# Top-k attention with a squared-ReLU MLP on one core: the first pair's loads and transposes, the timing of the weight loads, and identity products on TensorE

## The chip, the cores and the metric

One core of one Trainium2 chip runs the whole program. The metric is the device time of one execution in microseconds (us); the kernel before took 872.97 us, the median of three runs (872.86 to 874.77). The profile comes from one further execution of 870.8 us, whose traced span is 869.0 us. The engines are called as the profile calls them: PE (TensorE; PEld is its weight load), DVE (VectorE), ACT (ScalarE), POOL (GpSimd) and SP (SyncE, which here only issues DMAs).

## The reference

```python
# q, k, v: (8, 8, 576, 64) float32
scores = q @ k.transpose / sqrt(64)
kth = the 32nd largest score of each row
attn = softmax of the scores >= kth, the others left out
x = (attn @ v), heads side by side: (4608, 512)
h = x @ w_in            # (512, 2048)
out = relu(h)**2 @ w_out    # (2048, 512) -> (4608, 512) float32
```

## The kernel before, in words

**Tiles.** Two heads make a *pair*; there are 8 batches of 4 pairs. A pair's q and k (576 rows each) are loaded as 128-row blocks with the two heads side by side (tiles rq and rk; four whole blocks and a rest of 64 rows, three DMAs each). PE transposes them (ten transposes, L447), and ACT copies the result from PSUM into one tile qk (L511 to L514). A *group* is 128 queries of both heads of a pair (or 64 rests of two pairs); there are 144 groups. For each group:

- PE makes the scores (eight matmuls, L444) in a three-bank PSUM buffer of which there is one, ps_s.
- ACT copies them to SBUF (tile s, L555), DVE takes pairwise maxima (three operations, L611 and L621, called the *pair operations* here), partly reading ps_s; PE's next scores wait for the second of them. One quarter of the maxima lies for a moment in another single PSUM buffer, ps_q, which ACT empties (L619).
- POOL makes the matching minima by integer additions and subtractions (L606).
- DVE finds the 32nd largest by rounds of eight maxima and replacements (L638, L642, last L645, which writes kth).
- ACT makes a steep ReLU mask w (L653), PE transposes the scores and adds the mask (nine transposes and nine matmuls, called *flips* here), ACT takes the exponential p (L687), PE multiplies with v (tile vb, which POOL casts from rv at L515), ACT, DVE and POOL divide by the sum, and PE transposes the result into xt. The ninth block of the flips lies in ps_q too.

When all heads of 128 or 256 tokens are there, the MLP of this chunk is run: win matmuls, ReLU on ACT (L768), square on POOL, ACT or, for the last chunk, DVE (L779), wo matmuls, and an output DMA of 256 KB (L810).

**Weights.** w_in and w_out come as 16 float32 loads of 512 KB on SP's queue (L891) into two staging buffers, and are cast to bf16 by ACT or POOL (L894). All 16 may start from 6 us of the plan on (WN); how far apart they then come is set by their due times and the two buffers.

**Order.** A planner written in Python (class Plan, method schedule) simulates the five engines with an estimated duration for each operation, and at each moment starts on each engine the ready operation with the smallest due time (prio). Its result is the fixed order of each engine's list, and an Emitter adds semaphore waits. nbf is the earliest planned start of an operation; it puts no wait into the program. A planned load occupies SP for 0.6 us per DMA. The due times follow from the group's number and from a list of constants: PER and T0 (pace and start of the groups), LEAD (how far ahead scores are due), ME, MQ, MA, MP (pair operations, ACT's copy, POOL's operations), TA, TL, NL (attention, and how far it is pulled ahead over the last NL groups), LAG, LAGL, STEP (MLP), LATE (reciprocals). A second plan, for rows with special ties, stands behind a flag and isn't run.

**The start.** The first pair's q is issued on SP (three DMAs), its k on ACT's queue (three DMAs), then v (five DMAs) and the first weights on SP. Small POOL operations make a float32 and a bf16 identity and other constants.

```python
# the first pair's loads (in load_pair), and the transposes of every pair
pl.op("sp", 2.3, base - 80, load(rq, q, (512, 512)), w=[rq], take=[rq], sem=slot_sem, ndma=3)
via = "act" if not full and not state["pairs"] else None
pl.op("sp", 2.3, base - 79.9, load(rk, k, REST, nc.scalar if via else nc.sync), w=[rk], take=[rk], ...
o_q = pl.op("pe", .48, base - 45, t4(tq, rq), r=[rq], w=[tq], take=[tq, qk])
pl.op("pe", .48, base - 44.9, t4(tk, rk), r=[rk], w=[tk], take=[tk], order=[o_q])
```

Of the kernel before, what the change touches and what calls it, by code (L numbers as in the profile page):

```python
# [8 lines left out]
FP32 = mybir.dt.float32  # L9
# [67 lines left out]
class Op:  # L77
    __slots__ = ("eng", "dur", "prio", "fn", "deps", "tiles", "takes", "n", "users", "start", "end",
                 "idx", "sem", "val", "ndma", "seq", "vc", "waits", "wars", "later", "nbf", "lk", "late",
                 "via")  # L80


ENGS = ("pe", "act", "dve", "gp", "sp")
# [2 lines left out]
class Plan:  # L86
    def __init__(self):
        self.ops = []

    def op(self, eng, dur, prio, fn, r=(), w=(), u=(), hold=(), take=(), after=(), order=(), sem=None, ndma=0, nbf=0.0, lk=False, late=0.0, via=None):  # L90

        o = Op()
        o.eng, o.dur, o.prio, o.fn = eng, dur - (.1 if eng == "act" else 0), prio, fn
        o.sem, o.ndma, o.seq, o.nbf, o.lk, o.late, o.via = sem, ndma, len(self.ops), nbf, lk, late, via
        o.takes = list(take)
        o.users = []
        o.start = o.end = o.idx = o.val = o.vc = None  # L100
        deps = set(after)
        for t in r:
            deps.update(t.writers)
        for t in u:
            deps.update(t.ops)
        for t in list(r) + list(w) + list(u) + list(hold):
            t.ops.append(o)
            t.left += 1
        for t in list(w) + list(u):
            t.writers.append(o)  # L110
        for t in o.takes:
            t.taker = o
        o.later = ({t.taker for t in list(r) + list(w) + list(u) + list(hold)} | set(order)) - deps - {o, None}
        o.deps = deps
        o.wars = list(w) + list(u)
        o.tiles = list(r) + list(w) + list(u) + list(hold)
        self.ops.append(o)
        return o

    def schedule(self, t0=0.0, latency=0.12, own=0.07):  # L120
# [24 lines left out]
        while events:  # L145
            t = events[0][0]
            while events and events[0][0] <= t + 1e-9:
                _, _, kind, x = heapq.heappop(events)
                if kind == "end":
                    done += 1  # L150
                    for tl in x.tiles:
                        tl.left -= 1
                        if tl.left == 0 and tl.slot is not None:
                            for i in range(tl.width):
                                tl.pool.last[tl.slot + i] = tl
                            tl.pool.give(tl.slot, tl.width)
                    for v in x.users:
                        left[v] -= 1
                        lat = 0 if x not in v.deps else (own if x.eng != "pe" else .25) if v.eng == x.eng else latency
                        readyat[v] = max(readyat[v], t + lat)  # L160
                        if left[v] == 0:
                            push(readyat[v] + v.late, "ready", v)
                elif kind == "ready":
                    heapq.heappush(ready[x.eng], (x.prio, x.seq, x))
            for e in ENGS:
                if busy[e] > t + 1e-9 or (e == "gp" and locked > t + 1e-9):
                    continue
                skipped = []
                while ready[e]:
                    item = heapq.heappop(ready[e])  # L170
                    o = item[2]
                    got = []
                    ok = True
                    for tl in o.takes:
                        s = tl.pool.take(tl)
                        if s is None:
                            ok = False
                            break
                        got.append((tl, s))
                    if not ok:  # L180
                        for tl, s in got:
                            tl.pool.undo(s, tl.width)
                        skipped.append(item)
                        continue
                    for tl, s in got:
                        tl.slot = s
                        tl.prev = []
                        for i in range(tl.width):
                            p = tl.pool.last[s + i]
                            if p is not None:  # L190
                                tl.prev.append(p)
                    o.start = max(t, busy["gp"]) if o.lk else t
                    hold = o.dur if e != "sp" else 0.6 * o.ndma
                    o.end = o.start + o.dur + (hold if e == "sp" else 0)
                    busy[e] = o.start + hold
                    if o.lk:
                        locked = o.end
                    order[e].append(o)
                    push(busy[e], "go", None)
                    push(o.end, "end", o)  # L200
                    break
                for item in skipped:
                    heapq.heappush(ready[e], item)
# [88 lines left out]
def bass_top_k_attn__then__act_relu_squared_kernel(  # L292
# [22 lines left out]
    def sb(name, shape, dt=FP32, n=None):  # L315
# [3 lines left out]

    PER = 5.55  # L320
    T0 = 12.0
    LEAD = 40
    ME = 16.41
    MQ = 15.52
    MP = 18.0
    MA = 18.98
    SQ = 5.15
    TA = 7.2
    TW = -0.14
    TL = 8.0  # L330
    NL = 28.07
    WD = 3.33
    WC = 1.75
    WA = 1.13
    WN = 6
    NBO = 3.81
    LAG = 11.28
    STEP = 3.19
    LATE = 2.38
    LAGL = 11.07  # L340

    ident32 = sb("ident32", [P, P])
    ident_bf = sb("ident_bf", [P, P], BF16)
# [15 lines left out]


    sizes = {
        "rq": ([P, 5, 2, D], FP32, 2), "rk": ([P, 5, 2, D], FP32, 2), "rv": ([P, 12, D], FP32, 2),
        "qk": ([P, 2 * S + 64], FP32, 5), "vb": ([P, 12, D + 1], BF16, 5),
        "s": ([P, 2, S], FP32, 6), "m": ([P, 2, HALF], FP32, 3), "t1": ([P, 2, HALF], FP32, 2),
        "t2": ([P, 2, QUART], FP32, 2), "f": ([P, 2, S], FP32, 4), "a": ([P, 2, 8], FP32, 2),
# [20 lines left out]
    def tile(nm):  # L386
        return Tile(pools[nm])
# [63 lines left out]
    def build(full, weights, pl):  # L451
# [3 lines left out]
        def slot_sem(o):  # L455
            t = o.takes[0]
            return f"{t.pool.name}{t.slot}"

        def load_pair(b, hp, base):
            rq, rk, rv = tile("rq"), tile("rk"), tile("rv")  # L460


            def load(t, src, rest, queue=nc.sync):
                def fn():
                    r = at(t)
                    res = []
                    for h in range(2):
                        r0 = 64 if h and rest != (512, 512) else 0
                        res.append(queue.dma_start(r[:, 0:4, h, :], src[b, 2 * hp + h, r0:r0 + 512, :].rearrange(
                            "(tb p) d -> p tb d", p=P)))  # L470
                    x = src[b, 2 * hp, rest[0]:rest[0] + 64, :]
                    res.append(queue.dma_start(r[0:64, 4, :, :], bass.AP(
                        x.tensor, x.offset, [x.ap[0], [(S + rest[1] - rest[0]) * D, 2], x.ap[1]])))
                    return res
                return fn

            def loadv():
# [4 lines left out]
                for h, low, e in ((0, 0, 8), (1, 64, 9), (1, 0, 10) if hp % 2 == 0 else (0, 64, 11)):  # L482
                    res.append(nc.sync.dma_start(r[low:low + 64, e, :], v[b, 2 * hp + h, REST[h]:REST[h] + 64, :]))
                return res

            pl.op("sp", 2.3, base - 80, load(rq, q, (512, 512)), w=[rq], take=[rq], sem=slot_sem, ndma=3)
            via = "act" if not full and not state["pairs"] else None
            state["pairs"] += 1
            pl.op("sp", 2.3, base - 79.9, load(rk, k, REST, nc.scalar if via else nc.sync), w=[rk], take=[rk], sem=slot_sem,
                  ndma=3, via=via)  # L490
            pl.op("sp", 2.3, base - 70, loadv, w=[rv], take=[rv], sem=slot_sem, ndma=5)
            qk, vb = tile("qk"), tile("vb")
            tq, tk, tx = Tile(psum), Tile(psum), Tile(psum)

            def t4(o, src):
# [330 lines left out]
        for b in range(NB):  # L826
# [3 lines left out]
            for hp, gi in seq:  # L830
                tg = T0 + PER * state["n"]
                hps = (hp, hp if gi != Z else hp + 1)
                for x in hps:
                    if x not in pairs:
                        pairs[x] = load_pair(b, x, tg)
                st, wt = top_k(gi, [pairs[x][0] for x in hps], tg)
                tt = tg + PER + 2 - TA - TL * max(0, 1 - (NGRP - state["n"]) / NL)
                pt = attend(gi, st, wt, tt)
                js = [gi] if gi == Z else [g for g in stages if gi in g][0]
# [16 lines left out]
    def setup(pl):  # L856
# [22 lines left out]
        for i in range(16):  # L879
            s = tile("ws")  # L880
            if i < 8:
                half, ct = divmod(i, NCT)
                src = wi[:, ct, 1024 * half:1024 * half + 1024]
                dst = win[:, ct, 1024 * half:1024 * half + 1024]
                view = lambda s: at(s)[:, :]
            else:
                fb = 2 * (i - 8)
                src = wo_ap[:, fb:fb + 2, :]
                dst = wo[:, fb:fb + 2, :]
                view = lambda s: at(s)[:, :].rearrange("p (f o) -> p f o", f=2)  # L890
            pl.op("sp", 4.0, WD * i - 60, lambda s=s, src=src, view=view: [nc.sync.dma_start(view(s), src)],  # L891
                  w=[s], take=[s], ndma=1, sem=lambda o: f"ws{o.takes[0].slot}", nbf=WN)
            eng, fn = ("act", act.copy) if i % 4 < WA else ("gp", gp.tensor_copy)
            weights.append(pl.op(eng, 1.1, WC * i, lambda s=s, dst=dst, view=view, fn=fn: fn(dst, view(s)), r=[s]))  # L894
        return [i1], pre, zeros, weights

    def verdict(pl, kths, rzs):
# [103 lines left out]
```

## Time and profile before

| what | value |
|---|---|
| median of three runs | 872.97 us (872.86 to 874.77) |
| profiled execution, its span | 870.8 us, 869.0 us |
| busy PE / DVE / ACT / POOL | 809.9 / 822.5 / 760.3 / 788.2 us |
| instructions on PE / DVE | 7911 / 3413 |
| DMA, mean over the span | 55 GB/s |
| first operation of PE / DVE | 5.91 / 12.51 us |
| issue of the last weight load | 68.0 us |
| start of the last matmuls that make an output (15 recorded, 3.40 us) | 858.70 us |

The page gives the busy share of each engine in 40 slices of the span, the chain of work that ended last (followed back from the last instruction to what released each step), and groups of equal instructions. The table of stages gives the busy time of each engine between two moments. The list of waits says which engine stood idle until which other engine's instruction ended: total us, number of waits and the longest. A line of the timeline has the start, the length, the engine, the source line, the operation with output and input, and in brackets the idle time ahead of it and what ended it. Ends of matmuls are modelled, so a busy PE need not be PE at its peak.

### The profile page before, as it was taken

Reading aid. Unit: us, or ns where it says so; the run is one execution under the profiler, and the core shown is the slowest. Engines: PE = TensorE matmul, PEld = TensorE weight load, DVE = VectorE, ACT = ScalarE, POOL = GpSimd, SP = SyncE. Lnnn points to the kernel's source line nnn. Section 1 sums busy time; section 2 is a strip of 40 time slices with the busy share of each in tenths; the row PEclk is TensorE's granted clock in tenths of the full one; section 3 lists DMA queues with packets and bytes.
Section 4 is the critical chain, followed back from the end, with each engine's and each line's share of the span. In section 5 each row is a group of like instructions: output and inputs, shape, how many; then the busy total and the mean of one; then the engine's idle time right before and its main releaser. Section 6 shows DMA issues by size and latency. Waiting matters only on the chain.

```text
span 869.0 us, 22447 instructions
## 1 busy us (share of the span) xinstructions
PE 809.9 (93%) x7911; PEld 612.7 (71%) x7970; DVE 822.5 (95%) x3413; ACT 760.3 (87%) x1261; POOL 788.2 (91%) x826
## 2 busy tenths in 40 slices
PE   5777999989999999998999999999999999999996
PEld 3555777757687777766878677777777767677784
DVE  2989999999999999999999999999999999999971
ACT  4787998989898899989989799889999889898973
POOL 6898999999999998999999889998999987999971
PEclk9899999999999999999999999999999999999999
DMA  7881212131210223012131022202121021100000
GB/s 176 210 231 49 56 29 69 28 85 26 55 43 14 67 56 77 21 38 58 29 87 26 25 60 59 74 13 56 44 68 42 14 52 43 41 2 14 26 25 31
DMA packets 126969, 48.21 MB, mean 55 GB/s; under 512 B 119168, under 2 KB 119168, under 8 KB 126848
## 3 DMA queue, kind: packets, MB, share of 16 engines
q1 hardware_dynamic: 125648, 46.39, 21.3%
q8 instruction: 65, 1.06, 0.5%
q14 instruction: 56, 0.46, 0.2%
q10 hardware_dynamic: 1200, 0.30, 0.2%
HBM read 37.22 MB, written 9.44 MB: 54 GB/s over the span
## 4 chain that ended last, share of the span: by engine, by line
DVE 64%; PE 17%; ACT 11%; issue 4%; POOL 1%; DMA 1%; SPq 0%; DVEq 0%
DVE f L642 21%; DVE c L638 16%; PE ps L444 13%; DVE kth L645 13%; DVE f L621 5%; PE ps L447 5%; DVE ps L611 5%; DVE m L611 4%; ACT s L555 3%; ACT p L687 3%; ACT w L653 1%; ACT g L768 1%; POOL f L606 1%; POOL t L606 1%; DVE rzall L716 1%
## 5 line engine op out<-in xcount | busy, mean ns | idle before, releaser
L642 DVE MATCH_REPLACE8 f<-c,f 128x104 f32<-128x104 f32 (+2 forms) x864 | 272.2, 325 | 0.0
L638 DVE MAX8 c<-f 128x8 f32<-128x104 f32 (+2 forms) x864 | 248.8, 329 | 0.0
L447 PE MATMUL ps<-ident,s 128*128 128x128 f32 x1296 | 223.1, 281 | 21.5 <-ACT p L687 14.7
L653 ACT ACTIVATE w<-s,kth 128x576 bf16<-128x576 f32 x288 | 222.8, 786 | 19.8 <-DVE kth L645 18.5
L444 PE MATMUL ps<-qk 64*128 64x64 f32 (+3 forms) x1280 | 214.2, 454 | 10.2 <-DVE m L611 8.8
L606 POOL TENSOR_TENSOR t<-s 128x576 int32<-128x576 int32 x144 | 202.5, 1411 | 13.2 <-ACT s L555 13.1
L645 DVE MAX8 kth<-f 128x8 f32<-128x576 f32 x288 | 209.5, 757 | 0.0
L606 POOL TENSOR_TENSOR f<-t,m 128x576 int32<-128x576 int32 x144 | 203.2, 1411 | 0.1
L444 PEld LDWEIGHTS ps<-qk 64*128 64x128 f32 (+1 forms) x1280 | 132.6, 181 | 86.6 <-issue 62.9
L555 ACT COPY s<-ps 128x1152 f32<-128x1152 f32 x144 | 161.5, 1121 | 34.7 <-PE ps L444 33.7
L447 PEld LDWEIGHTS ps<-ident,s 128*128 128x128 f32 x1296 | 144.3, 142 | 48.0 <-ACT p L687 23.6
L687 ACT ACTIVATE p<-ps 128x1152 bf16<-128x1152 f32 x144 | 163.3, 1134 | 8.7 <-PE ps L444 7.8
L444 PE MATMUL ps<-steep_bf,w 128*128 128x128 bf16 x1296 | 141.1, 220 | 0.0
L606 POOL TENSOR_TENSOR t<-m 128x288 int32<-128x288 int32 x144 | 115.0, 799 | 19.3 <-ACT m L619 14.7
L444 PE MATMUL ps<-wo,g 128*128 128x512 bf16 x517 | 127.9, 379 | 4.0 <-issue 1.1
L444 PE MATMUL ps<-xt,win 128*128 128x256 bf16 (+1 forms) x1152 | 126.6, 261 | 1.5 <-ACT qk L511 0.8
L606 POOL TENSOR_TENSOR f<-t,f 128x288 int32<-128x288 int32 x144 | 114.9, 798 | 0.0
L444 PEld LDWEIGHTS ps<-xt,win 128*128 128x128 bf16 x1152 | 97.9, 98 | 15.9 <-ACT g L768 1.2
L444 PEld LDWEIGHTS ps<-steep_bf,w 128*128 128x128 bf16 x1296 | 106.0, 101 | 4.2
L782 POOL TENSOR_TENSOR g<-g 128x512 bf16<-128x512 bf16 x92 | 95.7, 1042 | 12.9 <-ACT g L768 11.7
L768 ACT ACTIVATE g<-ps 128x512 bf16<-128x512 f32 x144 | 86.0, 606 | 10.1 <-PE ps L444 9.3
L611 DVE TENSOR_TENSOR ps<-ps,s 128x288 f32<-128x288 f32 x144 | 66.6, 462 | 22.1 <-ACT s L555 17.1
(60 smaller groups left out, 882.4 us busy)
## 6 DMA issues: line engine op xcount, KB each, us to landing
rq<-in_q_dram SPq DMA_DIRECT2D x64, 128.0 KB, 2.5
rv<-in_v_dram SPq DMA_DIRECT2D x64, 128.0 KB, 2.4
out_dram<-o SPq DMA_DIRECT2D x32, 256.0 KB, 2.1
rk<-in_k_dram SPq DMA_DIRECT2D x62, 128.0 KB, 2.6
g<-in_moe_w_in_dram SPq DMA_DIRECT2D x8, 512.0 KB, 4.3
g<-in_moe_w_out_dram SPq DMA_DIRECT2D x8, 512.0 KB, 4.3
rv<-in_v_dram SPq DMA_DIRECT2D x96, 16.0 KB, 2.1
rq<-in_q_dram SPq DMA_DIRECT2D x32, 32.0 KB, 2.5
```

What stands on the lines that cost most here:

```text
L444: return pe.matmul(o, l, r, start=start, stop=stop, skip_group_check=True)
L447: return pe.matmul(o, i, ident, is_transpose=True, skip_group_check=True, **kw)
L555: cp = [pl.op("act", 1.2, tg - LEAD + 1, lambda: act.copy(at(st)[:, :, :], two(banks(ss), SECOND, S)), r=[ss], w=[st])]
L606: return pl.op("gp", dur, prio, lambda: gp.tensor_tensor(o().bitcast(I32), x().bitcast(I32), y().bitcast(I32), op), **kw)
L611: return vec.tensor_tensor(o, two(banks(ss)[:, a:], SECOND + HALF, QUART), two(at(st)[:, 0, HALF + a:], HALF, QUART), ALU.max)
L638: lambda i=i, t=t, c0=c0, c1=c1: vec.max(eighth(t, i), at(f)[:, i, c0:c1]),
L642: lambda i=i, t=t, c0=c0, c1=c1: vec.match_replace(at(f)[:, i, c0:c1], eighth(t, i), at(f)[:, i, c0:c1], NEG), hold=[f])]
L645: ks.append(chain(kth, i, prev[i] + [low], .665, lambda i=i: vec.max(eighth(kth, i), at(f)[:, i, :]), hold=[f]))
L653: pl.op("act", .77, tw + .8 * i, lambda i=i: act.activation(at(wt)[:, i, :], at(st)[:, i, :], ACTF.Relu, bias=kth[:, i, n:n + 1], scale=-1.0),
L687: pl.op("act", 1.15, tt + 1, lambda: act.activation(at(pt)[:, :, :].rearrange("p k q -> p (k q)"), banks(e)[:, 0:2 * S], ACTF.Exp, scale=0 ...
L768: return act.activation(at(g)[:, 0:kf * nt], bank(hh)[:, 0:kf * nt], ACTF.Relu)
L782: pl.op("gp", .15 + w_ / 480, tf + lag + 1, lambda g=g: gp.tensor_tensor(at(g)[:, 0:w_], at(g)[:, 0:w_], at(g)[:, 0:w_], ALU.mult), u=[g])
```

## The change

- The first pair is loaded otherwise (load_first). On ACT's queue: k of head 0 (four blocks) and the rests of k, two DMAs. On SP: k of head 1; block 0 of q, both heads, 64 KB; then the other q blocks and rests in three DMAs into a second q tile. v follows as before. The pool of q tiles has three instead of two.
- The first pair's transposes (first_pair): first q's block 0, then k's four blocks, then k's rest. DVE instead of ACT copies k's four blocks to qk; ACT copies q's block 0 and k's rest. The transposes of the other q blocks, their copy and the cast of v are put into the plan behind the first group's operations.
- The planner counts SP as occupied by a load for the larger of 0.6 us per DMA and a given bw: 1.9 us for each q, k or v load, 2.5 us for a weight load; loads on ACT's queue no longer occupy SP in the plan.
- Weight load i may start in the plan at 6 + 6.49 i us rather than at 6 us.
- 87 *identity products*: matmuls of the bf16 identity with itself, 128 x 512, into a free bank of the two-bank PSUM pool; nobody reads them. They have the last due time of all, and earliest planned starts 0.22 us apart up to 8 us (36 of them) and then 1.2 us apart up to 70 us (51). They wait for the bf16 identity and for the bank's last reader.
- Constants of the due times, as below.

The lists that result: PE has seven products, q's first transpose, two products, k's five, one product, the scores of group 1, q's other transposes, eight products, scores 2, then 22 products and the second pair's ten transposes ahead of scores 3, flips 1, eight products and scores 4. In DVE's list the first two pair operations of group 3 come after all of group 1 and all of group 2 but its last kth; before, they came ahead of group 1's two kth. In the last stretch of PE's list the last win matmuls stand together (96, after a piece of 32) ahead of 32 wo matmuls, where before it was 64 and 16.

```diff
-    LEAD = 40
-    ME = 16.41
-    MQ = 15.52
+    LEAD = 39.88
+    ME = 21.85
+    MQ = 19.61
...
-    MA = 18.98
+    MA = 18.27
...
-    TL = 8.0
-    NL = 28.07
+    TL = 18.33
+    WARM = 8
+    WP = 6.49
+    BW = 1
+    WSTEP = 1.2
+    WEND = 70
+    NL = 31.89
...
-    LAG = 11.28
-    STEP = 3.19
-    LATE = 2.38
-    LAGL = 11.07
+    LAG = 12.93
+    STEP = 2.98
+    LATE = 2.07
+    LAGL = 17.86
...
-                    hold = o.dur if e != "sp" else 0.6 * o.ndma
+                    hold = o.dur if e != "sp" else max(o.bw, 0.6 * o.ndma * (o.via is None))
...
-        "rq": ([P, 5, 2, D], FP32, 2), "rk": ([P, 5, 2, D], FP32, 2), "rv": ([P, 12, D], FP32, 2),
+        "rq": ([P, 5, 2, D], FP32, 3), "rk": ([P, 5, 2, D], FP32, 2), "rv": ([P, 12, D], FP32, 2),
...
+            pl.op("sp", .1, base - 82, start(nc.scalar, lambda: part(rk, k, 0, 0, 4),
+                                             lambda: rest(rk, k, REST[0], REST[1] - REST[0])),
+                  w=[rk], take=[rk], sem=slot_sem, ndma=2, via="act")
+            pl.op("sp", 2.3, base - 81, start(nc.sync, lambda: part(rk, k, 1, 0, 4)), w=[rk], sem=lambda o: "first", ndma=1)
+            pl.op("sp", 2.3, base - 80, start(nc.sync, lambda: (at(rq)[:, 0, :, :], both)), w=[rq], take=[rq],
+                  sem=slot_sem, ndma=1)
+            pl.op("sp", 2.3, base - 79, start(
+                nc.sync, lambda: part(rq2, q, 0, 1, 3), lambda: part(rq2, q, 1, 1, 3), lambda: rest(rq2, q, 512, 0)),
+                w=[rq2], take=[rq2], sem=slot_sem, ndma=3)
...
+            o_x = pl.op("pe", .15, base - 45.2, flips(tx, rq, [0]), r=[rq], w=[tx], take=[tx, qk])
+            o_k = pl.op("pe", .5, base - 45.1, flips(tk, rk, [0, 1, 2, 3]), r=[rk], w=[tk], take=[tk], order=[o_x])
...
+            pl.op("act", .3, base - 42.5, lambda: act.copy(at(qk)[:, 0:128], bank(tx)[:, 0:128]), r=[tx], w=[qk])
+            pl.op("dve", .6, base - 42.5, lambda: vec.tensor_copy(at(qk)[:, 640:1152], bank(tk)), r=[tk], w=[qk])
...
+            def later():
+                pl.op("pe", .5, base - 44, flips(tq, rq2, [1, 2, 3, 4]), r=[rq2], w=[tq], take=[tq])
+                pl.op("act", .6, base - 42, lambda: act.copy(at(qk)[:, 128:576], bank(tq)[:, 0:448]), r=[tq], w=[qk])
+                pl.op("gp", .8, base + 5, lambda: gp.tensor_copy(at(vb)[:, :, 0:D], at(rv)[:, :, :]),
+                      r=[rv], w=[vb], take=[vb])
...
             pl.op("sp", 4.0, WD * i - 60, lambda s=s, src=src, view=view: [nc.sync.dma_start(view(s), src)],
-                  w=[s], take=[s], ndma=1, sem=lambda o: f"ws{o.takes[0].slot}", nbf=WN)
+                  w=[s], take=[s], ndma=1, sem=lambda o: f"ws{o.takes[0].slot}", nbf=WN + WP * i, bw=BW * 2.5)
...
+        times = [.22 * i for i in range(int(WARM / .22))]
+        times += [WARM + WSTEP * i for i in range(int((WEND - WARM) / WSTEP))]
+        for x in times:
+            t = Tile(psum)
+            pl.op("pe", .22, 1e5, lambda t=t: mm(bank(t), ident_bf[:, :], ident_bf[:, :].unsqueeze(1).broadcast_to(
+                [P, 4, P]), True), w=[t], take=[t], after=[i2], nbf=x)
```

## The prediction

> **What bounds the kernel now.** I read the busy tenths first, then the chain that ended last, then a table of stages, and last the waits of VectorE (DVE) by stage and the instructions of the first 40 us. From the page:
>
> ```profile
> DVE  2989999999999999999999999999999999999971
> ...
> DVE 64%; PE 17%; ACT 11%; issue 4%; POOL 1%; DMA 1%; SPq 0%; DVEq 0%
> ```
>
> DVE is full in nearly every slice but the first two and the last, and carries 64% of the chain. The table of stages (busy us of PE, PEld, DVE, ACT, POOL with counts, then clock, DMA share, GB/s):
>
> ```profile
> 0.00:12.50 12.50, 4.84 (x18) 3.44 (x18) 0.00 (x0) 3.86 (x6) 5.11 (x31) 1.00 0.85 183
> 12.50:35.00 22.50, 16.59 (x78) 12.09 (x80) 17.10 (x68) 14.19 (x24) 19.14 (x19) 1.00 0.82 198
> 35.00:70.00 35.00, 25.35 (x205) 19.72 (x202) 32.20 (x129) 30.39 (x48) 31.80 (x33) 0.85 0.80 211
> 70.00:120.00 50.00, 45.38 (x450) 34.89 (x449) 48.47 (x204) 43.64 (x74) 45.83 (x47) 0.97 0.13 32
> 120.00:830.00 710.00, 686.11 (x6784) 517.75 (x6836) 709.75 (x2957) 647.44 (x1073) 671.14 (x680) 1.00 0.18 44
> ```
>
> From 120 to 830 us DVE idles 0.25 us of 710. So nothing in the middle can be gained except by giving DVE less work, which the change doesn't do. DVE's idle time before that is 12.5, 5.4, 2.8 and 1.5 us, 22.2 us together. The waits of DVE from 13 to 120 us name what it waited for:
>
> ```profile
> DVE ps L611 <- ACT p L687: 4.8, 6, 1.3
> DVE ps L611 <- ACT s L555: 4.5, 3, 2.7
> DVE f L621 <- ACT m L619: 0.3, 1, 0.3
> ```
>
> Behind "s" stands TensorE (PE): ACT's copy s waits for the scores. The instructions of PE show two speeds for the same eight score matmuls:
>
> ```profile
> 13.39 2.50 PE L444 MATMUL ps<-qk 64*128 64x64 f32 x8 [2.08 <-DVE m L611]
> ...
> 34.58 1.35 PE L444 MATMUL ps<-qk 64*128 64x64 f32 x8 [2.29 <-DVE m L611]
> ```
>
> The first four groups (8.81, 13.39, 18.74, 23.32 us), the seventh (38.95) and one at 71.20 took about 2.5 us, the others near 1.35. The last stage: DVE's last threshold (kth) ends at 840.58 us and the span at 869.0; PE's work from the last scores (825.77) to its last matmul (862.1) leaves almost no gap, so the end is PE's.
>
> [...] Here an issue of the first loads takes 0.5 to 0.76 us.
>
> **The change, part by part.** Each step is a change of DVE's idle time or of the tail.
>
> *A. First scores.* Before, the scores at 8.81 wait for all of q and k: q's third DMA is issued at 1.79 and lands at 5.9, then ten transposes and four ACT copies. After, two k DMAs go on ACT's queue, one k and one q block (64 KB) on SP's. The last of these starts at about 1.3 instead of 1.9 us, and 352 KB instead of 576 KB (216, 232 and 286 GB/s in busy parts of the first 30 us; at 216 that is 1.0 us less) stand ahead. I take both landed at 4.9 us, 1.0 earlier. Against it stand the added identity products. They need the bf16 identity, ready at 2.0 us; seven stand ahead of q's transpose, 7 x 0.43 cold = 3.0, so until 5.0. Then one transpose (0.3), two products (0.86), four k transposes (1.06, as at 6.79) and the rest (0.3): 7.5. DVE's new copy of k (128x512, no such row; between its 288-element PSUM operation of 0.47 and its 576-element maximum of 0.76, I take 0.6) and ACT's two small copies (0.25 each) end at 8.1. Scores start at 8.2. PE will have worked 6 us by then, so I take it warm: 1.35, copy s 1.12, handovers 0.1: the first pair operation of DVE at 10.8 instead of 12.51, **1.7 us**. If the first scores are still cold it is 0.6; if the loads land at 4.3 and the clock wakes early, 2.7. The copy of k lies in DVE's idle time.
>
> *B. The next groups (12.5 to 35 us).* DVE's idle there is 2.72 ahead of group 2, then 0.26, 0.94, 0.88 and 0.45: 5.25. Warm scores give each of the cold groups 1.15 back. Group 2: DVE's pair ends at 11.65, but PE's new order has q's remaining transposes (0.66) and eight products (1.8) there, so scores 2 start at 12.0, s lands at 14.6, and DVE, having run dry at 12.6, idles 2.0. Group 3: PE's order has 22 products (4.8 us) and ten transposes (1.6) between; scores 3 at 19.9, s at 22.4. But the order of DVE puts all of group 1 and all of group 2 but a kth ahead of that pair, work until about 23.5, so no wait. Eight products before scores 4 may cost 0.5. Idle of 2.5 instead of 5.25: **2.75 us**, from 0 (products too long) to 4.5.
>
> *C. The p waits and the loads (35 to 120 us).* DVE idles 4.3 there. Its "p" waits mean that the single PSUM buffer shared by the pairs and the exponent's end came free late, when PE and ACT ran late: PE waited for k until 45.02 after a load of 4.2 us, and a cast of weights stood on the chain at 33.67, 35.39 and 48.79. The 16 loads (one DMA of 0.59 us issue each on SP, one cast of 1.04 each on ACT or POOL) remain, but load i starts no sooner than 6 + 6.49 i us by plan, the last at 103 rather than 68; SP's plan counts 2.5 us for each rather than 0.6. DMA share falls below 0.8, casts come singly, and q has a third buffer. Who waits for late weights: the MLP, whose first activation is at 97.7 and first wo matmul at 118.7; the last cast at about 103 + 4.3 + 1.04 = 108 is ahead of it. The order agrees: after 40 score groups the MLP has done 3 win pieces in both kernels and 4.25 instead of 5 wo blocks. I take half of 4.3, **2.0 us** (0 to 4). SP's queue: ten DMAs instead of eight stand up to the end of v, about 0.85 us later for v, the first weights and pair 2. V's cast on POOL now stands behind group 1's four operations, and PE takes pair 2 no sooner than 16 us. That hides it.
>
> *D. Due times.* LEAD, ME, MQ, TL, LAG and the others only move work. In the middle DVE has the same instructions per group, so 0, with 3 us either way where an order no longer fits. In the tail I summed PE's row durations backwards. Before: 36.0 us from the last scores, which follow a DVE pair 15.5 us of DVE work ahead of the last kth, a tail of 20.5 (21.5 measured). After: 39.8 and 20.5, a tail of 19.3: **1.2 us**, between a loss of 2 and a gain of 3.
>
> *E. The other products.* 87 in all. 51 of them are spread one per 1.2 us to 70 us, 0.22 to 0.43 each. PE's idle time up to 70 us is 70 - 46.8 = 23.2 us, and 87 x 0.22 = 19. Waiting for a PSUM bank or standing ahead of a score I charge **1.0 us** (0 to 14, see the first rival).
>
> Sum: 1.7 + 2.75 + 2.0 + 1.2 - 1.0 = 6.65 us of a span of 869.0. That run took 870.8; the runs' median is 872.97, from which I take it: 866.3.
>
> **The rivals.**
> 1. *Products that jam PE.* PE runs its list in order; a product whose bank is not evacuated, or that runs cold, holds the scores behind it. For: 40 stand ahead of scores 3. Against: PE idles 23 us there. It decides from the point where products exceed the idle time: all cold, 87 x 0.43 = 37, 14 beyond it. With A, C and D (4.9) still gained: 872.97 + 14 - 4.9 = 882, half of that excess 875. Chance 0.11.
> 2. *PE becomes the bound.* It is 97% busy from 120 to 830 (24 us idle). An earlier DVE then only waits longer, the tail grows by what the start gives: 872. Against: modelled ends exaggerate it, and DVE never waited. Chance 0.13.
> 3. [...] Chance 0.14.
> 4. *All start waits go and the tail gains 3*: A 2.7, B 4.5, C 4, D 3, less 1: 860. Chance 0.06.
> My forecast, 863 to 869: 0.56.
>
> **How the numbers follow.** About 0.3%, 2.6 us, is what a measurement can tell from no change. Faster than 870.35: the forecast, case 4 and over half of case 3: 0.70. Same: most of case 2 and the rest of 3: 0.18. Slower: case 1 and a little of 2, 0.12. The range runs from 861.5 to 872.5; outside lie case 1, half of case 4 and a little of case 2.
>
> **What would show it.** Right: DVE's first pair near 10.8; score matmuls of 1.35 us from the first or second group on; at most 6 us of DVE idle from 12.5 to 120; none from 120 to 830; last kth near 835, tail near 27. Wrong: scores of 2.5 us after 15 us, PE waiting ahead of ident_bf products, DVE waits in the middle, or a tail over 29.

## The result, and the profile after

The changed kernel took 869.43 us (median of four runs, 868.93 to 870.16), the kernel before 872.91 us (871.69 to 874.77). The ratio is 0.9959 with a 95% interval of 0.994 to 0.9978: faster by 0.4%. The profiled execution has a span of 867.1 us, against 869.0 before. The execution profiled before was 2.1 us shorter than the median, so the two spans are 1.9 us apart where the medians are 3.5 apart. What follows compares the spans.

The page of the kernel after, the same two lines as before:

```profile
DVE  3899999999999999999999999999999999999970
...
DVE 66%; PE 21%; ACT 8%; issue 5%; POOL 1%; DVEq 0%; POOLq 0%
```

The table of stages of the kernel after (PE, PEld, DVE, ACT, POOL busy us, clock, DMA share, GB/s):

```profile
0.00:12.50 12.50, 9.44 (x35) 3.59 (x35) 2.41 (x6) 3.73 (x7) 6.29 (x32) 1.00 0.70 158
12.50:35.00 22.50, 20.59 (x123) 11.51 (x123) 17.04 (x69) 14.27 (x23) 17.41 (x18) 1.00 0.69 160
35.00:70.00 35.00, 32.27 (x276) 21.32 (x272) 33.07 (x140) 29.22 (x47) 31.37 (x33) 1.00 0.66 165
70.00:120.00 50.00, 42.94 (x409) 30.98 (x411) 49.98 (x207) 46.30 (x75) 46.76 (x48) 1.00 0.37 100
120.00:830.00 710.00, 689.82 (x6822) 520.91 (x6876) 709.67 (x2956) 649.45 (x1080) 673.78 (x684) 1.00 0.17 43
```

DVE's idle time is now 10.1, 5.5, 1.9 and 0.02 us up to 120 us; before it was 12.5, 5.4, 2.8 and 1.5. That is 4.7 us less, of which DVE's new copy of k (0.69 us) takes a part back. The middle is as full as it was. The stage from 12.5 to 35 us, where every score group now takes 1.34 or 1.35 us, has gained nothing.

Scores of 2.50 us are called cold and scores of 1.35 us warm here. The granted clock goes with that only in part: in the kernel before it was 0.50 from 38.95 to 41.4 us, during scores of 2.50 us, and 1.00 from 30.12 to 31.4, during scores of 1.34; but it was also 1.00 from 13.39 to 15.82, during scores of 2.50. That a clock makes the first four groups slow is thus not shown.

DVE's last kth ends at 836.27 us instead of 840.58, 4.3 us sooner. In the timeline of DVE, before and after:

```profile
839.17 1.41 DVE L645 MAX8 kth<-f 128x8 f32<-128x576 f32 x2
```

```profile
834.85 1.42 DVE L712 MAX8 kth<-f 128x8 f32<-128x576 f32 x2
```

But from there to the end of the span it is 30.8 us instead of 28.4 (called *the rest* below). So between these two executions 2.4 of the 4.3 us are given back at the end. The 28.4 us come from one execution, and a short one; what the rest is in a median execution of the kernel before no profile shows.

DVE's waits from 13 to 35 us in the kernel after, and PE and DVE in the timeline around there:

```profile
DVE ps L678 <- ACT s L622: 4.2, 2, 3.1
DVE ps L678 <- ACT p L754: 1.4, 1, 1.4
```

```profile
9.85 3.09 PE L449 MATMUL ps<-ident_bf 128*128 128x512 bf16 x8
...
12.87 1.35 PE L449 MATMUL ps<-qk 64*128 64x64 f32 x8
...
21.87 1.34 PE L449 MATMUL ps<-qk 64*128 64x64 f32 x8
...
26.07 0.47 DVE L678 TENSOR_TENSOR ps<-ps,s 128x288 f32<-128x288 f32 x1 [1.40 <-ACT p L754]
```

DVE's pair operations of group 1 have left the score buffer by about 11.3 us, but scores 2 start at 12.87, behind eight identity products that take 3.0 us. Scores 3, behind 22 more and ten transposes, start at 21.87; group 1's flips stand behind them, its exponential ends at 26.0, and only then is the small PSUM buffer free for DVE's next pair.

### The profile page after: what moved, and what is told of

Read it like the earlier page. It is cut to its first block, busy times and chain, and to the rows that moved or that the text cites. A ratio compares the mean times of both kernels' runs of the same rounds, so it can differ in the third digit from the quotient of the medians.

```text
span 867.1 us, 22631 instructions
## 1 busy us (share of the span) xinstructions
PE 823.6 (95%) x7998; PEld 609.9 (70%) x8057; DVE 824.2 (95%) x3414; ACT 760.2 (88%) x1261; POOL 788.2 (91%) x826
## 4 chain that ended last, share of the span: by engine, by line
DVE 66%; PE 21%; ACT 8%; issue 5%; POOL 1%; DVEq 0%; POOLq 0%
DVE f L709 21%; DVE c L705 17%; PE ps L449 15%; DVE kth L712 13%; PE ps L452 5%; DVE ps L678 5%; DVE f L688 5%; DVE m L678 5%; ACT p L754 2%; ACT w L720 1%; ACT s L622 1%; ACT g L835 1%; DVE rzall L783 1%; ACT qk L579 0%; ACT g L852 0%
## 5 line engine op out<-in xcount | busy, mean ns | idle before, releaser
L709 DVE MATCH_REPLACE8 f<-c,f 128x104 f32<-128x104 f32 (+2 forms) x864 | 268.1, 317 | 0.0
L705 DVE MAX8 c<-f 128x8 f32<-128x104 f32 (+2 forms) x864 | 244.7, 321 | 0.1
L449 PE MATMUL ps<-qk 64*128 64x64 f32 (+3 forms) x1280 | 207.0, 442 | 2.9 <-DVE m L678 2.5
L449 PEld LDWEIGHTS ps<-qk 64*128 64x128 f32 (+1 forms) x1280 | 128.1, 175 | 77.4 <-issue 60.4
L449 PEld LDWEIGHTS ps<-wo,g 128*128 128x128 bf16 x576 | 51.8, 98 | 48.5 <-ACT g L835 0.5
```

Of the source, the lines that this page charges most:

```text
L449: return pe.matmul(o, l, r, start=start, stop=stop, skip_group_check=True)
L705: lambda i=i, t=t, c0=c0, c1=c1: vec.max(eighth(t, i), at(f)[:, i, c0:c1]),
L709: lambda i=i, t=t, c0=c0, c1=c1: vec.match_replace(at(f)[:, i, c0:c1], eighth(t, i), at(f)[:, i, c0:c1], NEG), hold=[f])]
```

## The experiments

Each verdict rests on the ratio to the kernel before, run beside it, with its 95% interval. Medians of different rows come in part from different chips, so the ratios are what compares. Each reading rests on one profiled execution; these lie within 1 us of their kernel's median, but for the kernel before (2.1 us shorter), e1_tiny (1.4 longer) and e4_weights (3.5 longer). "Last kth" is the end of DVE's last MAX8 into kth. The diffs show the lines that matter; "..." marks what is left out.

| kernel | ratio (95%) | median us | last kth | rest |
|---|---|---|---|---|
| before | 1 | 872.91 | 840.6 | 28.4 |
| changed | 0.9959 (0.9940 to 0.9978) | 869.43 | 836.3 | 30.8 |
| e1_tiny | 1.0002 (0.9988 to 1.0016) | 872.81 | 841.6 | 30.7 |
| e5_few | 0.9950 (0.9935 to 0.9965) | 868.54 | 835.7 | 30.6 |
| e6_nowait | 0.9911 (0.9896 to 0.9926) | 865.47 | 833.0 | 30.6 |
| e7_tail | 0.9989 (0.9978 to 0.9999) | 871.42 | 838.0 | 31.4 |
| e3_due | 1.0000 (0.9981 to 1.0018) | 872.51 | 838.3 | 32.6 |
| e4_weights | 1.0058 (1.0040 to 1.0076) | 876.65 | 847.4 | 30.9 |
| e8_first | 1.0011 (0.9997 to 1.0024) | 872.86 | 839.9 | 31.3 |
| e9_products | 1.0012 (0.9998 to 1.0026) | 872.83 | 840.1 | 30.5 |
| e12_dueonly | 1.0092 (1.0069 to 1.0115) | 880.50 | 847.2 | 32.4 |
| e10_half | 0.9933 (0.9913 to 0.9954) | 865.92 | 832.4 | 30.9 |
| e11_less | 0.9932 (0.9906 to 0.9959) | 864.99 | 831.6 | 30.6 |

### The products without their work: e1_tiny

```diff
-mm(bank(t), ident_bf[:, :], ident_bf[:, :].unsqueeze(1).broadcast_to([P, 4, P]), True)
+mm(bank(t)[:, 0:8], ident_bf[:, :], ident_bf[:, 0:8], True)
```

> All lists as in the changed kernel, but each of the 87 identity products has 8 columns instead of 512, so it keeps its place and its waits and takes almost no PE time. Theory 'the warm clock pays': the score matmuls of the first groups take 2.5 us again, DVE's first pair operation comes at 11.0 us or later, DVE idles 6 to 9 us from 12.5 to 70 us, and the time is 2 to 4 us above the changed kernel's. Rival 'the products give back what the clock brings': the scores are slow too, but scores 2 and 3 no longer stand behind 8 and 22 products of 0.22 to 0.45 us; DVE idles no more than the 7.4 us it idled from 12.5 to 70, and the time is within 1 us of the changed kernel's.

The scores are slow again; here the second group, from the timeline of PE:

```profile
12.30 2.50 PE L449 MATMUL ps<-qk 64*128 64x64 f32 x8
```

The first four groups all took 2.5 us, DVE idled 11.4 us from 12.5 to 70 us instead of 7.4, and the last kth came 5.3 us later. Warm scores pay: without them the rest of the change is worth nothing (1.0002). The granted clock of the stage from 12.5 to 35 us is 1.00 here as in the changed kernel, though three groups in it took 2.5 us, so this run shows what the products' columns are worth, and not that a clock stands behind it. The first theory stands in its direction and its time. Its figure for the first pair was off (10.85 us, since less stood ahead of scores 1), and so was that for DVE's idle time, which is longer than the 6 to 9 us expected. The products were not free here: the eight ahead of scores 2 still took 1.6 us, since each still waited.

### Fewer products ahead of scores 2 and 3: e5_few

```diff
...
+n_ = 8 if 11 <= made[0] <= 40 else 512
...
```

Here n_ is the number of columns of product number made[0].

> All lists as in the changed kernel; only products 11 to 40, the 8 ahead of scores 2 and the 22 ahead of scores 3, have 8 columns. Theory 'these 30 products cost DVE its waits for groups 2 and 3': scores 2 start when DVE's pair ends (11.3 instead of 12.9 us), scores 3 near 18 instead of 21.9, the wait of 1.4 us for the exponential near 26 us goes, and the last kth comes 2 to 3 us sooner; the clock may fall back to scores of 2.5 us for two or three groups, which takes back up to 1.2 us each. Rival 'the loads of pair 2 and ACT set scores 3 anyway': the last kth moves by less than 0.7 us. Theory 'DVE sets the end': the time falls by as much as the last kth moves. Rival 'PE's backlog sets the end': the last kth moves, the tail after it (30.8 us) grows by as much, the time stays within 0.7 us.

From the timeline of PE, the eight thin products ahead of scores 2, and scores 3:

```profile
10.34 1.62 PE L449 MATMUL ps<-ident_bf 128*128 128x8 bf16 x8
...
19.27 2.50 PE L449 MATMUL ps<-qk 64*128 64x64 f32 x8
```

Scores 2 started at 11.89, still warm (1.35 us), and scores 3 at 19.27, but cold (2.50 us); the granted clock of the stage from 12.5 to 35 us is 0.77 instead of 1.00. DVE's idle time from 12.5 to 35 us fell from 5.5 to 4.5 us, while its first pair came at 10.93 instead of 10.44, though nothing ahead of it had been edited. The wait for the exponential did not go, and the last kth moved by 0.6 us, not by 2 to 3: the size that the first rival named, though scores 3 did come 2.6 us sooner. So the 30 products do hold scores 2 and 3, and their columns are also what keeps scores 3 at 1.35 us: making them thin is no cure. On the end the run shows no backlog of PE: the rest is 30.6.

### Products that don't wait for one another: e6_nowait

```diff
+        self.products = set()
...
                         deps.add(x)
+            if o in self.products:
+                deps -= self.products
...
```

> All lists as in the changed kernel; a product no longer waits for the product before it in the same PSUM bank (PE runs its list in order, and nobody reads either). Theory 'a good part of the products' time is the wait for one another' (PE stood idle 14.0 us in 39 waits for its own earlier instruction ahead of products): the 8 products ahead of scores 2 take 1.8 instead of 3.0 us, scores 2 start near 11.7, the 6 ahead of pair 2's k take 1.3 instead of 2.0; DVE gains 1.2 to 2 us by its last kth. Rival: the time between products of one bank is PE's own and stays 0.45 us; nothing moves. At the end, as before: either the time falls by as much as the last kth, or the tail takes it up.

From the view of the bf16 identity's instructions up to 75 us, PE's own row in the list of what their engine stood idle for ahead of them (us, times): first the changed kernel, then this one. The row counts the weight loads (PEld) ahead of the products: these stood idle for 14.0 us until an earlier matmul had ended, not PE itself, as the expectation has it. In PE's timeline the same wait shows as the time from one product to the next.

```profile
  PE ps L449: 14.0, 39
```

```profile
  PE ps L452: 0.6, 1
```

The same eight products and scores 2 in the timeline of this kernel:

```profile
10.01 1.90 PE L452 MATMUL ps<-ident_bf 128*128 128x512 bf16 x8
11.84 1.35 PE L452 MATMUL ps<-qk 64*128 64x64 f32 x8
```

Eight products take 1.8 us instead of 3.0, scores 3 start at 19.81 instead of 21.87, and DVE's wait for the exponential is 0.4 us. The last kth comes 3.3 us sooner and the span ends 3.5 us sooner. The theory was right and its size too small; the rival, that the 0.45 us are PE's own, is refuted. This kernel is faster than both: its interval lies below the changed kernel's.

### The due times at the end: e7_tail

```diff
-    TL = 18.33
+    TL = 8.0
...
-    NL = 31.89
+    NL = 28.07
...
-    LAGL = 17.86
+    LAGL = 11.07
```

> TL, NL and LAGL as before the change (8.0, 28.07, 11.07); the lists differ only over the last third. Theory 'the new due times lengthened the tail': with the last kth near 836.3 as in the changed kernel, the tail is 28.4 us as before the change and the time falls by about 2.4 us to 867. Rival 'an earlier DVE meets a PE that is not earlier': the tail stays at 30 to 31 us or longer, whatever the due times, and the time is within 0.7 us of the changed kernel's or above it.

The rest is 31.4, not 28.4, and the last kth comes 1.7 us later, with a new wait of DVE of 1.5 us between 120 and 830 us. These three constants did not lengthen the rest: with the changed kernel's other values the old ones are worse. Why the rest stays long is not shown by this run.

### All due times as before, or alone: e3_due and e12_dueonly

e3_due takes the whole constants part of the change's diff back except WARM, WP, BW, WSTEP and WEND; e12_dueonly puts just that part into the kernel before. The first of the ten lines, for e3_due:

```diff
-    LEAD = 39.88
+    LEAD = 40
...
```

> All ten due-time constants (LEAD, ME, MQ, MA, TL, NL, LAG, STEP, LATE, LAGL) as before the change; the new loads, weight timing and products stay. The head of PE's list is the same. Theory 'the new due times moved the end of the chain from PE to DVE and are needed for the gain': the last kth comes within 2 us of 836.3, but the rest after it is longer than 31 us, or DVE waits again from 70 us on, and the time is 871 us or more. Rival 'the new due times only lengthened the rest after the last kth from 28.4 to 30.8 us': without them it is 28.4 again and the time is 867.

> The kernel before with the ten new due-time constants alone. Theory 'the rest after the last kth belongs to the new due times': it is 30 to 31 us instead of 28.4 while the last kth stays within 1 us of 840.6, so the time rises by about 2 us to 875. Rival 'the new due times pull PE's end forward by themselves, as the summing of PE's list said': the rest is 27 to 28 us, the time 871.5 or less. If instead the last kth comes later by over 1 us, the new due times don't suit the old loads, and the rest tells nothing by itself.

With the old due times, the new loads, weight timing and products together are worth nothing (1.0000): the start is the same, DVE idles 2.5 us more from 70 to 120 us, and the rest is 32.6. The new due times alone, on the other hand, lose 0.9%: DVE idles 6.7 us from 12.5 to 35 us and 3.8 from 35 to 70, and 2.2 from 120 to 830 us. This is the third outcome named beforehand; its rest (32.4) tells nothing by itself. The due times are needed for the gain, and they need the rest of the change.

### The weight loads as before: e4_weights

```diff
-    WP = 6.49
-    BW = 1
+    WP = 0
+    BW = 0
```

> Weight loads planned as before the change (all from 6 us on, 0.6 us of SP per DMA); products, first loads and due times stay. Theory 'the spread loads took DVE's waits from 35 to 120 us away': DVE idles about 4 us there again instead of 2.0, the last kth comes 2 us later, the time is about 871.4. Rival 'the warm clock did it': DVE idles at most 2.5 us there, the time is within 1 us of 869.4.

The chain of this kernel around 41 us and PE's waits from 35 to 70 us:

```profile
41.60 6.08 DMA rk<-in_k_dram
```

```profile
PE ps L452 <- DMA rk<-in_k_dram: 3.9, 2, 2.7
```

DVE idles 7.7 us from 35 to 70 us, more than in either kernel. One k of a pair, issued 1.7 us after a weight load, takes 6.08 us to land (the median of k's loads is 2.5), PE stands for it, and so does what is behind it in the list. That the weight load is what delays it is argued from the order of the issues, not shown by itself. The direction of the first theory is right and its size (2 us) far too small: by the ratios (1.0058 against 0.9959) the spread loads are worth 1.0% in this kernel, about 8.6 us; by the last kth of the profiled execution, which was a long one, 11.

### One part on the kernel before: e8_first and e9_products

e8_first is the changed kernel with the edits of e3_due and e4_weights and this one:

```diff
-        times += [WARM + WSTEP * i for i in range(int((WEND - WARM) / WSTEP))]
+        times = []
+        [WARM + WSTEP * i for i in range(int((WEND - WARM) / WSTEP))]
         for x in times:
```

The list left standing on a line of its own is used by nobody, so no product is made.

e9_products has the change's loop over times, with its 87 products, in the kernel before.

> The first pair's loads and transposes alone (with the third q tile): no products, weight loads and due times as before the change. Theory 'the loads bring the first pair operation forward, whatever the clock': DVE's first pair near 11.0 us (scores at 7.3, cold, 2.5 us) instead of 12.51, so 1.5 of the 2.1 us of the whole change; the last kth 1 to 1.5 us sooner; time 871.5. Rival 'the cold groups that follow take it back': the last kth within 0.5 us of the 840.6 before, time 872.9.

> The kernel before with the 87 products alone. Theory 'warm scores shorten the start without the new loads too': scores of 1.35 us from the first group on; but 19 products stand ahead of the first pair's transposes, which start no sooner than 5.9 us, and 10 each ahead of scores 2 and 4, at 0.22 to 0.45 us; first pair operation within 0.7 us of 12.5, DVE's idle time from 12.5 to 120 us falls from 9.7 to 6 to 8; time 870 to 871.5. Rival 'without the loads brought forward the products hold the first scores': first pair operation at 13.3 or later, time 873 or more.

The loads alone bring DVE's first pair to 10.65 us, almost where the whole change has it (10.44), with scores of 2.5 us. The last kth moves by only 0.7 us and the time not at all: later waits take it back. The products alone make the first eleven score groups 1.35 us, but hold the first pair until 13.83; the time doesn't move either. By the time both rivals hold; by the last kth e8_first lies between its theory and its rival. Both have the old due times, and their rests are 31.3 and 30.5 us.

### Less ahead of the first scores: e10_half and e11_less

```diff
+n_ = 8 if 19 <= made[0] <= 40 and made[0] % 2 else 512
+n_ = 8 if 8 <= made[0] <= 10 or 19 <= made[0] <= 40 and made[0] % 2 else 512
```

Both have e6_nowait's edit too; the first line is e10_half's, the second e11_less's.

> As the kernel whose products don't wait for one another, and in addition every second one of the products 19 to 40 (ahead of scores 3) has 8 columns. Theory 'what stands ahead of scores 3 is still PE time of products': 11 x 0.2 = 2.2 us less, scores 3 near 18 instead of 19.8 us, the remaining wait of 0.4 us for the exponential goes; the last kth 0.3 to 0.8 us sooner, time about 865. Rival 'scores 3 no longer set DVE': nothing moves at the end, 865.5. If the clock falls back: above 866.

> As the kernel before it, and in addition the three products between q's first transpose and scores 1 have 8 columns. Theory 'they hold the first scores': scores 1 start near 7.3 instead of 8.0 us, DVE's first pair near 9.9, the last kth 0.5 to 0.7 us sooner than there. Rival 'seven products are not enough to wake the clock by then': scores 1 take 2.5 us, the first pair comes at 11.0, the time is above that of the kernel before it.

In e10_half scores 3 start at 19.03 (near 18 was expected), warm (1.34 us), the wait for the exponential is gone, and the last kth comes 0.5 us sooner than in e6_nowait. In e11_less, without the three products ahead of scores 1, these start at 7.12, warm (1.35 us), DVE's first pair comes at 9.67, and the last kth 0.8 us sooner still. In the times the three kernels can't be told apart (their intervals overlap); in the profiles the last kth moves as expected, and e11_less has the shortest span, 862.2 us.

## Why the prediction was right in its direction, and where its steps failed

The time lies in the range and the sign was right; the gain is 3.5 us where 6.65 was forecast (of the medians). The range is 11 us wide, and the time misses the likeliest part of it, 863 to 869, by 0.4 us: that it lies inside owes as much to that width as to the steps. Of the signs named beforehand, scores of 1.35 us, the first pair and a full middle came true. DVE's idle time from 12.5 to 120 us is 7.4 us, not at most 6, and two signs of being wrong showed: waits ahead of the products, and a tail over 29. Step by step, in the profiled spans:

- **A, first scores: 1.7 forecast, 2.1 measured** (first pair 10.44 instead of 12.51, with scores 1 at 7.89 taking 1.34 us). e8_first shows that the loads carry nearly all of it: 10.65 without products, with scores of 2.50 us. In the changed kernel the products ahead of scores 1 take back most of what the faster scores give; without three of them the first pair comes at 9.67 (e11_less). That 6 us of PE work make the scores warm was the author's assumption, and the sum of its work does not decide it: in the kernel before PE had been busy for 12.1 us when scores 4 started at 23.32, and they took 2.50 us; in the changed kernel it had been busy for 5.1 us when scores 1 started. No row of the kernel before shows the 0.43 us of a cold product that this step and E reckon with. In the changed kernel the first seven took 0.42 us each (2.06 to q's transpose at 5.00), and as much without waits for one another (to 5.02 in e6_nowait); later ones came 0.22 to 0.23 us apart without such waits.
- **B, groups 2 to 4: 2.75 forecast, nothing measured** (5.5 us idle instead of 5.4). The step priced "eight products (1.8)" and 22 products at 4.8 us by their work of 0.22 us. It did not see that a product waits not only for the bank's last reader but, where there is none, for the last product in the same bank, which is also PE's: 3.0 us for the eight. And "so no wait" for group 3 counted only its scores, not that group 1's flips stand behind them in PE's list, and the exponential's buffer behind the flips. e6_nowait showed both: with the waits gone, 2.0 of the 2.75 us are there (3.4 us idle), and the wait for the exponential falls from 1.4 to 0.4 us.
- **C, 35 to 120 us: 2.0 forecast, 2.4 measured** (4.3 to 1.95 us). The size was right, but the step gave it to the loads' timing alone. DVE's idle time there is 9.3 us without that timing (e4_weights), and it is back at 4.5 without the products' work (e1_tiny) and at 4.3 with the old due times (e3_due): all three are needed.
- **D, the tail: 1.2 gained in the forecast, 2.4 lost between the two profiled executions.** The step added PE's durations backwards as if PE were never without input. PE's work from the last scores was put at 39.8 us and took 41.6 (818.65 to 860.2), of which 1.9 us are waits for ACT; these scores started 1.0 us after DVE's pair had ended; and DVE's work from that pair to the last kth was 18.6 us, not 20.5.
- **E, the products' cost: 1.0 forecast.** It was mis-sized in the same way as B. The waits for one another ahead of products lay in part in PE's idle time; the part that did not cost 3.3 us by the last kth (e6_nowait): 2.1 of DVE's idle time in B's stage and 1.0 from 35 to 70 us.

The first rival, products that jam PE, was thus right in mechanism and in place, but by the wait for a product (0.45 us from one to the next) rather than by the products' own speed (0.22 to 0.23), and it cost 3.3 us, not 14. The third, by which products 1.2 us apart leave the scores cold, is refuted for the products as they ran, in bundles and beside PE's other work: every group of eight score matmuls up to 120 us took 1.34 or 1.35 us. The second, that PE becomes the bound, named what the two profiles show, a tail that takes back part of what the start gives; but PE did not become the bound. DVE idles only 0.3 us from 120 to 830 us. In the five kernels with the changed kernel's lists, or its lists but for the products' width or waits (e1, e5, e6, e10, e11), the last kth lies between 831.6 and 841.6 us and the rest between 30.6 and 30.9: the end follows DVE one for one. The chain of waits near the end agrees. DVE's last kth pieces and ACT's first piece in it, before and after:

```profile
822.09 0.68 DVE kth L645
822.80 0.78 ACT w L653
```

```profile
830.36 0.67 DVE kth L712
831.05 0.78 ACT w L720
```

Before, the chain leaves DVE at 822.8 us, 46 us ahead of the end, and runs through PE and ACT from there: DVE's last 18 us were not on it. After, it leaves DVE at 831.05, 36 us ahead of the end. That alone doesn't explain the rest: in e3_due and e9_products the chain leaves DVE at 822.5 and 815.8 us, and the rest is 32.6 and 30.5. What makes the rest 2.4 us longer stays open. e7_tail and e3_due, which put due times back, made it longer still, and e8_first and e9_products, with the old due times and a last kth within 0.7 us of the one before, have 31.3 and 30.5. Only the one profile of the kernel before has a rest under 30 us.

None of the three parts that were run alone gains: first loads 1.0011, products 1.0012, due times 1.0092. The change without the products' work (1.0002), the new due times (1.0000) or the weights' timing (1.0058) gains nothing. So the gain needs these together. The weights' timing alone, and the change without the new first loads, were not run.

## What to carry to other kernels

A filler instruction is priced by what it waits for, and not by its length alone (here 0.45 us from one to the next with a wait, 0.22 to 0.23 without): look for waits of an engine, or of its weight loads, for itself. Where a fixed order is planned from estimated times, one changed part takes the plan away from under the others, so price parts by shrinking an instruction in its place, with the lists unchanged, and not only by removing it. Before adding up the work behind the bounding engine's last step, see in the chain of waits where it leaves that engine.

## What the runs showed that had not been expected

A 512-column product that waits for the one before it in its bank comes 0.45 us after it; without the wait, 0.22 to 0.23 (2.9 us for 13 in the changed kernel where the banks alternate). Cutting a product to 8 columns doesn't remove the wait: the eight of e5_few still take 1.6 us. And little is needed to keep the scores at 1.35 us. Beside the kernel's own work, 51 products planned 1.2 us apart, which ran in bundles, held every score group at 1.35 us up to 70 us, where the kernel before, warm at 34.58 us (1.35), was slow again at 38.95 (2.50) and at 71.20 (2.47), and in part at 59.02 (1.74). The granted clock of the stages from 35 to 70 and from 70 to 120 us is 0.85 and 0.97 before and 1.00 in both after. With every second of the 22 ahead of scores 3 thin, these still ran at 1.35 us (e10_half); with all 22 and the eight before them thin, at 2.50 (e5_few).

Scores that turn cold again do not follow a long standstill of PE. In e5_few PE was never idle for more than 0.3 us at a stretch from scores 2 (1.35 us) to scores 3 (2.50), and in the kernel before never for more than 2.3 us from 30 to 38.95 us. What ran just ahead of the cold scores was transposes and, in e5_few, thin products too; which of them it is that fails to keep the scores at 1.35 us no run here separates.
